# Attention weights and products in PSUM banks of their own, the product with v one turn later, and the reciprocal moved to the middle of the step

## Chip, cores and metric

The kernel runs on one core of a Trainium2 chip. The metric is the device time of one execution in microseconds (us). Before the change it was 1007.72 us (median of three runs, 1006.71 to 1010.24).

## What is computed

The reference chains two blocks. The first is attention over 8 batches x 8 heads, 576 positions, head width 64, that keeps only the 32 largest scores of each row:

```
scores = scale * (q @ k.T)
kth    = the 32nd largest score of each row
attn   = exp(where(scores >= kth, scores, -1e9) - max);  attn /= attn.sum() + 1e-9
out    = attn @ v
```

Its output, read as 4608 tokens of width 512, goes into a mixture of eight experts: each token takes the expert with the largest gate logit, each expert keeps the 80 tokens with the largest gate weight, applies `relu(x @ w1) @ w2`, and multiplies by the gate weight. All other rows of the output are zero. The change touches the attention block only.

## The kernel before

**Units and tiles.** Attention works on 32 head pairs, one after the other. A head pair has five tiles of query rows: tiles 0 to 3 of 128 rows, for both heads, and tile 4 of the last 64 rows, in which both heads share the 128 partitions. A unit is one head of one tile, so a head pair has nine units: two for each of the tiles 0 to 3, one for tile 4.

**The loop.** `run` (L454) lays out the program by hand (`manual_schedule`): each engine executes its instructions in the order in which they are written, and waits when an operand or a buffer isn't ready. `step(i)` (L473) is called once for each unit i and writes:

1. The loads of later q, k and v (L476 to 479, on SP's queue).
2. A string of letters (L488), one string for odd and one for even i, that interleaves VectorE work on several units: `G` a maximum over a sixth of a row (L250); `a` to `e` the rounds of the search for the 24th largest candidate (L261, L269), the last of which, `e`, also issues ScalarE's sign of the row against that candidate (L266); `y` GpSimd's product of the row with the sign (L272); `g` VectorE's maximum over that (L274); `h`/`H` the pick of the threshold (L277); `m`/`M` the mask of values below the threshold (L288), which for odd units is a ScalarE instruction (L293) and for even units a GpSimd one (L295). `h H m M` stand only in the string of even steps. `z`/`Z` is the reciprocal of the row sums (`over`, L360) and `x`/`X` the division of the product by the sums (`divide`, L370): two ScalarE copies with a scale (L385), except for tile 3, where VectorE does it (L377).
3. `turn_w` (L314) of a whole tile: TensorE transposes its scores into PSUM (L333) and adds the masks times a huge negative number (L339); ScalarE takes the exponential, first of the tail (the 65th to 128th key of the last chunk, L342), then of the rest (L343), into `wT`. Called *the turn* and *the exponentials* below.
4. `front` (L224): q times k of a later tile on TensorE (L234), and ScalarE's copy of the scores to SBUF (L242).
5. `back` (L346): the product of `wT` with v on TensorE (L356; 20 matmuls for a tile of two heads, 10 for tile 4), where v has a column of ones, so that the sums come with it. Called *the product*.
6. In some steps one more TensorE job that needs the PSUM tile of `front`: the transposes of q and k of the next head pair (`turn`, L211, ScalarE copy at L222), or, for the gate, the transposes of a finished head pair (L400, ScalarE copy L402). The gate logits (L407, copied at L414) are written inside `turn_w`, between its transposes and its masks (`gate`, L518).

With s = i mod 9, the tiles of these jobs are, before the change:

| s | turn | front | product | reciprocal, division | other |
|---|---|---|---|---|---|
| 7 | 0 | 1 | | 4 (of the pair before) | |
| 8 | | | 0 | | |
| 0 | 1 | 2 | | 0 | |
| 1 | | | 1 | | q, k transposes |
| 2 | 2 | 3 | | 1 | |
| 3 | | | 2 | | gate transposes |
| 4 | 3, logits in it | 4 | | 2 | |
| 5 | 4 | 0 | 3, ahead of the turn | | |
| 6 | | | 4 | 3 | |

Within a step the letters come first, then turn, front, product. Since nine is odd, the parity of i at a given s changes from one head pair to the next: where step 7 is odd, so are 0, 2 and 4, and 8, 1, 3 and 5 are even (called an *odd pair* below); in the next head pair it is the other way round (an *even pair*).

**PSUM** has eight banks. `ps_s` (L203) holds one tile of four banks for `front`, the transposes of q and k, and the gate; each use waits until ScalarE has copied the one before. `ps_w` is one tile of two banks for the turned scores `ab`. `ps_c` has two tiles `cc` of one bank; one `cc` holds the turned tail in its first 128 columns and behind them the products and sums of the same tile (L323, L351), and so lives from the turn until the division.

Of the kernel before, what the change touches and what calls it, by code (L numbers as in the profile page):

```python
# [9 lines left out]
F32 = mybir.dt.float32  # L10
# [4 lines left out]
Act = mybir.ActivationFunctionType  # L15
# [8 lines left out]
TINY = 2.0 ** -48  # L24
# [3 lines left out]
def kernel(  # L28
# [120 lines left out]
    class Attention:  # L149


        def __init__(self, stack, lean):
            self.lean = lean
            pool = lambda name, bufs, **kw: stack.enter_context(tc.tile_pool(name=name, bufs=bufs, **kw))
            self.nat, self.qkp, self.rows = pool("nat", 1), pool("qkp", 2), pool("rows", 2)
            self.small, vpool = pool("small", 7), pool("vpool", 1)
            self.ps_s, self.ps_w, self.ps_c = (pool(n, k, space=PSUM) for n, k in (("ps_s", 1), ("ps_w", 1), ("ps_c", 2)))
            self.qk, self.turned, self.lg = {}, {}, {}
            self.s, self.top, self.cnt, self.y, self.mask, self.w, self.xn = ({} for _ in range(7))
            self.both_s = {}  # L160
            self.thr, self.z = thr_all, z_all
            self.odd = set()


            self.vb = []
            for j in range(1 if lean else 3):
                t = vpool.tile([P, 3 * NF + 4, D + 1], F32, name=f"vb{j}")
                nc.gpsimd.memset(t[:, :, D : D + 1], 1.0)
                nc.gpsimd.memset(t[TL:, 3 * NF, :], 0.0)
                nc.gpsimd.memset(t[:TL, 3 * NF + 1 :, :], 0.0)  # L170
                self.vb.append(t)

            self.xT = vpool.tile([P, NK * P], F32, name="xT")
            nc.gpsimd.memset(self.xT[:, S:], 0.0)
# [139 lines left out]
        def turn_w(self, n, t, between=None):  # L314

            i = n * UPP + 2 * t
            g = 2 if t < NF else 1
            if i == NU - 1 and not self.lean:

                ab = self.four().rearrange("p h (c r) -> p h c r", r=P)  # L320
            else:
                ab = self.ps_w.tile([P, 2, NF, P], F32, name="ab", tag="ab")
            cc = self.ps_c.tile([P, 512], F32, name="cc", tag="cc")  # L323


            keys = [slice(c * P, c * P + P) for c in range(2 * NF + 1)] if t < NF else [slice(c * P, c * P + P) for c in range(NF)] + [slice(S - P, S)]
            dst = [ab[:, 0, c, :] for c in range(NF)] + [cc[:, :P]] + ([ab[:, 1, c, :] for c in range(NF)] if t < NF else [])
            sc, mk = self.both_s.pop((n, t)), self.mask.pop((n, t))
            for h in range(g):
                self.s.pop(i + h)  # L330

            for c, o in enumerate(dst):
                nc.tensor.matmul(o, lhsT=sc[:, keys[c]], rhs=ident, start=c in (0, NF, NF + 1), stop=False, is_transpose=True,  # L333
                                 skip_group_check=True)
            if between:
                between()

            for c in sorted(range(len(dst)), key=lambda c: c != NF):
                nc.tensor.matmul(dst[c], lhsT=mk[:, keys[c]], rhs=minus if self.lean else huge, start=False, stop=True,  # L339
                                 skip_group_check=True)  # L340
            wT = self.rows.tile([P, 2 * NF + 1, P], F32, name="wT", tag="wT")
            nc.scalar.activation(wT[:, 2 * NF, :], cc[:, :P], Act.Exp, scale=scale / TINY)  # L342
            nc.scalar.activation(wT[:, : g * NF, :], ab.rearrange("p h c r -> p (h c) r")[:, : g * NF, :], Act.Exp, scale=scale / TINY)  # L343
            self.w[n, t] = wT, cc

        def back(self, n, t):  # L346

            wT, cc = self.w.pop((n, t))
            vb = self.vb[n % len(self.vb)]
            for h in range(2 if t < NF else 1):  # L350
                o = slice(P + h * (D + 1), P + (h + 1) * (D + 1))  # L351
                for c in range(NK):
                    for r in range(0, P, TL):
                        j = h if t < NF else 2 * r // TL
                        k = j * NF + c if c < NF else 3 * NF + (h if t < NF else 2 + r // TL)
                        nc.tensor.matmul(cc[r : r + TL, o], lhsT=wT[:, h * NF + c if c < NF else 2 * NF, r : r + TL],  # L356
                                         rhs=vb[:, k, :], start=(c == 0), stop=(c == NF))
            self.w[n, t] = cc

        def over(self, n, t):  # L360


            g = 2 if t < NF else 1
            sums = self.w[n, t][:, P : P + 2 * (D + 1)].rearrange("p (h d) -> p h d", h=2)[:, :g, D]
            z = self.z[:, n % NP, t, :g]
            if self.lean:
                nc.vector.tensor_scalar(z, sums, EPS, None, op0=Alu.add)
            nc.vector.reciprocal(z, z if self.lean else sums)  # L368

        def divide(self, n, t):  # L370
            if t == 0:
                self.xn[n] = self.rows.tile([P, NK, 2, D], F32, name="xn", tag="xn")
            cc = self.w.pop((n, t))
            if t == NF - 1:

                sums = cc[:, P : P + 2 * (D + 1)].rearrange("p (h d) -> p h d", h=2)[:, :, :D]
                nc.vector.tensor_tensor(out=self.xn[n][:, t, :, :], in0=sums, op=Alu.mult,  # L377
                                        in1=self.z[:, n % NP, t, :].unsqueeze(2).to_broadcast([P, 2, D]))
                return
            for h in range(2):  # L380
                if t < NF:
                    p, o, j, m = slice(0, P), P + h * (D + 1), h, P
                else:
                    p, o, j, m = slice(TL * h, TL * h + TL), P, 0, TL
                nc.scalar.activation(self.xn[n][:m, t, h, :], cc[p, o : o + D], Act.Copy, scale=self.z[p, n % NP, t, j : j + 1])  # L385

        def norm(self, n, b, hp, bi, nb, cs=range(NK)):
# [66 lines left out]
        def run(self, slow):  # L454
# [8 lines left out]
            first, second = {}, {}  # L463
            later = []
            due = []
            drawn = []
            ready = {}

            def whole(i):

                return 0 <= i < NU and units[i][2] > 0

            def step(i, last):  # L473
                if 0 <= i < NU:
                    n, t, h = units[i]
                    if t == 2 and h == 1 and n + 2 < NP:  # L476
                        self.load(n + 2, *divmod(n + 2, HP))
                    if t == 3 and h == 1 and n + 2 < NP:
                        self.load_v(n + 2, *divmod(n + 2, HP))
                    if t in (1, 3) and h == 0 and slow and n:  # L480
                        slow.pop(0)()
                    if t == 0 and h == 0 and n + 1 < NP:
                        due.append(n + 1)
                    first[i] = self.parts(i)


                lag = dict(a=0, b=1, c=1, d=1, e=1, y=3, g=4, h=5, m=5, H=4, M=4)
                for c in "GybGcZGdXGeGGzaxg" if i % 2 else "GGbghHmMyGcZGdXGeGzax":  # L488
                    if c == "G":
                        if 0 <= i < NU:  # L490
                            next(first[i])
                    elif c == "a":
                        if 0 <= i < NU:
                            next(first[i], None)
                            second[i] = self.search(i)
                            next(second[i])
                    elif c in "zZxX":
                        for n, t in drawn:
                            if (t == NF - 1) == (c in "ZX"):
                                (self.over if c in "zZ" else self.divide)(n, t)  # L500
                    elif c in "mM":
                        if 0 <= i - lag[c] < NU:
                            self.below(i - lag[c])
                    elif i - lag[c] in second:
                        next(second[i - lag[c]])
                done = list(drawn)
                drawn.clear()

                def back():
                    if whole(i - LT - 1):  # L510
                        self.back(*units[i - LT - 1][:2])
                        drawn.append(units[i - LT - 1][:2])


                rest = whole(i - LT) and units[i - LT][2] == 2
                if rest:
                    back()
                def gate():  # L518
                    for g in later:
                        if ready[g] == 2:  # L520
# [2 lines left out]
                if whole(i - LT):  # L523
                    self.turn_w(*units[i - LT][:2], gate)

                ends = [(n, range(NK) if n < NP - 1 else range(NF) if t < NF else range(NF, NK))
                        for n, t in done if t == NF or (n == NP - 1 and t == NF - 1)]

# [1 line left out]
                busy = 0 <= f < NU and units[f][2] != 1  # L530
                if busy:
                    self.front(*units[f][:2])
                if not rest:
                    back()
                if due and not busy and i > 0:
                    self.turn(due.pop())
                    busy = True
# [413 lines left out]
```

## Time and profile before

| | |
|---|---|
| median of three runs | 1007.72 us |
| profiled execution | 1008.7 us, of which the span from first to last instruction is 1007.0 us |
| TensorE matmul busy | 857.1 us |
| VectorE busy | 811.3 us |
| ScalarE busy | 774.0 us |
| GpSimd busy | 625.8 us |
| granted TensorE clock | 0.98 on average |

The attention loop fills the span from about 30 to 876 us; the rest is routing and the experts. In the stretch from 500 to 600 us VectorE is busy for 91.32 us, ScalarE for 90.18 and TensorE for 87.23. Three engines are thus nearly full, and what counts is which waits for which. Three views tell it: the list of waits (who sat idle until whom, in total us, times and longest), the timeline of one engine in a window (start, length, line, and in brackets the idle time just before it with its releaser), and the groups by line. The release of a wait by an engine that is itself late tells where to look next.

### The profile page before, as it was taken

Reading aid. Unit: us, or ns where it says so; the run is one execution under the profiler, and the core shown is the slowest. Engines: PE = TensorE matmul, PEld = TensorE weight load, DVE = VectorE, ACT = ScalarE, POOL = GpSimd, SP = SyncE. Lnnn points to the kernel's source line nnn. Section 1 sums busy time; section 2 is a strip of 40 time slices with the busy share of each in tenths; the row PEclk is TensorE's granted clock in tenths of the full one; section 3 lists DMA queues with packets and bytes.
Section 4 is the critical chain, followed back from the end, with each engine's and each line's share of the span. In section 5 each row is a group of like instructions: output and inputs, shape, how many; then the busy total and the mean of one; then the engine's idle time right before and its main releaser. Section 6 shows DMA issues by size and latency. Waiting matters only on the chain.

```text
span 1007.0 us, 35335 instructions
## 1 busy us (share of the span) xinstructions
PE 857.1 (85%) x13112; PEld 690.6 (69%) x13112; DVE 811.3 (81%) x4960; ACT 774.0 (77%) x1588; POOL 625.8 (62%) x477
## 2 busy tenths in 40 slices
PE   5888898898888898888888888887888887689997
PEld 3666677676766677667666667666676676578886
DVE  5898999999898989898999999998999899361110
ACT  3889888898889898989898888898898989500110
POOL 3677677767677677677677776776767767301111
PEclk9999999999999999999999999999999999878999
DMA  3554443333323333333222221222221200183921
GB/s 86 129 140 125 131 131 91 89 97 97 98 76 85 96 93 86 98 97 77 55 56 55 56 54 45 51 50 56 56 55 44 58 22 14 33 316 127 388 73 31
DMA packets 189813, 91.00 MB, mean 90 GB/s; under 512 B 139712, under 2 KB 176576, under 8 KB 189632
## 3 DMA queue, kind: packets, MB, share of 16 engines
q1 hardware_dynamic: 188608, 86.03, 30.8%
q0 software_dynamic: 1024, 2.62, 0.8%
q8 instruction: 105, 1.72, 0.7%
q14 instruction: 76, 0.62, 0.2%
HBM read 68.44 MB, written 20.19 MB: 88 GB/s over the span
## 4 chain that ended last, share of the span: by engine, by line
PE 38%; ACT 25%; DVE 23%; issue 8%; POOL 3%; DMA 2%; POOLq 0%; ACTq 0%; DVEq 0%; SPq 0%
PE cc L356 12%; ACT sign L266 9%; DVE cand L250 7%; PE sp L234 6%; ACT wT L343 6%; DVE w L274 5%; PE sp L209 5%; ACT mask L293 4%; PE yp L835 4%; DVE cand L269 3%; ACT xn L385 3%; PE ab L333 3%; POOL y L272 3%; DVE top L261 2%; ACT wT L342 1%
## 5 line engine op out<-in xcount | busy, mean ns | idle before, releaser
L250 DVE MAX8 cand<-s 128x8 f32<-128x96 f32 x1728 | 400.2, 246 | 8.7 <-ACT s L242 8.7
L295 POOL TENSOR_SCALAR mask<-s,thr_all 128x576 bf16<-128x576 f32 x144 | 247.9, 1721 | 243.5 <-DVE pick L277 148.0
L272 POOL TENSOR_TENSOR y<-s,sign 128x576 f32<-128x576 f32 x288 | 363.1, 1281 | 12.7 <-ACT sign L266 12.7
L356 PEld LDWEIGHTS cc<-vb,wT 128*64 128x64 f32 x5760 | 184.1, 139 | 180.0 <-ACT wT L343 168.9
L356 PE MATMUL cc<-vb,wT 128*64 128x65 f32 x5760 | 206.5, 226 | 110.7 <-ACT wT L343 110.7
L274 DVE MAX8 w<-y 128x8 f32<-128x576 f32 x288 | 217.1, 754 | 14.6 <-POOL y L272 7.5
L266 ACT ACTIVATE sign<-s,w 128x576 bf16<-128x576 f32 x288 | 223.1, 775 | 6.6 <-DVE w L261 6.1
L234 PE MATMUL sp<-both 64*128 64x288 f32 (+1 forms) x1280 | 203.3, 437 | 9.8 <-ACT s L242 4.5
L242 ACT ACTIVATE s<-sp 128x1152 f32<-128x1152 f32 (+1 forms) x161 | 166.9, 1037 | 34.0 <-PE sp L234 32.6
L333 PE MATMUL ab<-ident,s 128*128 128x128 f32 x1148 | 178.7, 285 | 0.0
L343 ACT ACTIVATE wT<-ab 128x1024 f32<-128x1024 f32 (+1 forms) x159 | 149.9, 942 | 3.4 <-PE ab L339 3.2
L234 PEld LDWEIGHTS sp<-both 64*128 64x128 f32 (+1 forms) x1280 | 106.3, 180 | 51.0 <-ACT s L242 7.9
L333 PEld LDWEIGHTS ab<-ident,s 128*128 128x128 f32 x1148 | 130.1, 144 | 11.7 <-issue 0.8
L261 DVE MAX8 top<-cand 128x8 f32<-128x48 f32 x576 | 115.2, 200 | 5.6
L293 ACT ACTIVATE mask<-s,thr_all 128x576 bf16<-128x576 f32 x144 | 111.7, 776 | 8.3 <-DVE pick L277 7.9
L269 DVE MATCH_REPLACE8 cand<-top,cand 128x48 f32<-128x48 f32 x576 | 110.9, 192 | 0.0
L339 PE MATMUL ab<-huge,mask 128*128 128x128 bf16 x1148 | 91.2, 221 | 0.0
L339 PEld LDWEIGHTS <-mask 128*128 128x128 bf16 x1312 | 84.2, 99 | 7.2 <-issue 5.2
L368 DVE RECIPROCAL z_all<-cc 128x2 f32<-128x2 f32 (+1 forms) x160 | 25.8, 162 | 59.9 <-PE cc L356 59.9
L385 ACT ACTIVATE xn<-cc,z_all 128x64 f32<-128x64 f32 (+1 forms) x256 | 68.0, 306 | 1.6 <-DVE z_all L368 1.2
L222 ACT COPY both<-sp 128x1152 f32<-128x1152 f32 x31 | 34.8, 1123 | 30.0 <-PE sp L209 30.0
L342 ACT ACTIVATE wT<-cc 128x128 f32<-128x128 f32 x160 | 44.4, 278 | 17.0 <-PE cc L339 14.1
(187 smaller groups left out, 853.2 us busy)
## 6 DMA issues: line engine op xcount, KB each, us to landing
w<-in_moe_w_dram SPq DMA_DIRECT2D x10, 2048.0 KB, 12.3
vb<-in_v_dram SPq DMA_DIRECT2D x96, 128.0 KB, 2.7
w<-in_moe_w_dram SPq DMA_DIRECT2D x24, 512.0 KB, 3.8
out_dram<-zero SPq DMA_DIRECT2D x9, 1024.0 KB, 5.8
qn<-in_q_dram SPq DMA_DIRECT2D x64, 128.0 KB, 2.5
kn<-in_k_dram SPq DMA_DIRECT2D x64, 128.0 KB, 2.5
xd<-xn SPq DMA_DIRECT2D x32, 256.0 KB, 2.6
qn<-in_q_dram SPq DMA_DIRECT2D x32, 32.0 KB, 2.3
```

The costliest lines, as they stand in the source:

```text
L234: nc.tensor.matmul(o, lhsT=qT[d, t * P : t * P + m], rhs=kT[d, j * HS : (j + 1) * HS], start=True, stop=True)
L242: nc.scalar.activation(s[:, j * HS : (j + w) * HS].rearrange("p (j c) -> p j c", c=HS), ps[:, j : j + w, :HS], Act.Copy, scale=TINY)
L250: nc.vector.max(out=cand[:, j, :], in_=s[:, j * S // NG : (j + 1) * S // NG])
L266: nc.scalar.activation(sign, s, Act.Sign, bias=w9[:, 7:8], scale=-1.0, accum_out=cnt)
L272: nc.gpsimd.tensor_tensor(out=y, in0=s, in1=sign, op=Alu.mult)
L274: nc.vector.max(out=w9[:, 8:], in_=y)
L293: nc.scalar.activation(mask, self.s[i], Act.Relu, bias=self.thr[:, i : i + 1], scale=-1.0)
L295: nc.gpsimd.tensor_scalar(mask, self.s[i], self.thr[:, i : i + 1], None, op0=Alu.is_lt)
L333: nc.tensor.matmul(o, lhsT=sc[:, keys[c]], rhs=ident, start=c in (0, NF, NF + 1), stop=False, is_transpose=True, skip_group_check=True)
L339: nc.tensor.matmul(dst[c], lhsT=mk[:, keys[c]], rhs=minus if self.lean else huge, start=False, stop=True, skip_group_check=True)
L343: nc.scalar.activation(wT[:, : g * NF, :], ab.rearrange("p h c r -> p (h c) r")[:, : g * NF, :], Act.Exp, scale=scale / TINY)
L356: nc.tensor.matmul(cc[r : r + TL, o], lhsT=wT[:, h * NF + c if c < NF else 2 * NF, r : r + TL], rhs=vb[:, k, :], start=(c == 0), stop=(c = ...
```

## The change

- PSUM: the tail of the turn gets a pool and a bank of its own (`ps_t`, tile `tt`). `cc` now holds products and sums only, is allocated in `back`, and has one bank instead of two.
- `back` of a tile is written behind the next tile's `turn_w` and ahead of the step's `front`, by way of the list `turned`. The special case that put `back` ahead of the turn in step 5 is gone.
- The letters: `Z` and `X` are gone. For all tiles, `z` stands after the fourth `G` and `x` after the next one in even steps, and after the third and fourth `G` in odd steps. `e` moves behind the last `G`.
- The v of a later head pair is loaded one step later.

With these the table reads:

| s | turn | product | front | reciprocal, division | other |
|---|---|---|---|---|---|
| 7 | 0 | 4 (of the pair before) | 1 | | |
| 8 | | | | 4 (of the pair before) | |
| 0 | 1 | 0 | 2 | | |
| 1 | | | | 0 | q, k transposes |
| 2 | 2 | 1 | 3 | | |
| 3 | | | | 1 | gate transposes |
| 4 | 3, logits in it | 2 | 4 | | |
| 5 | 4 | 3 | 0 | 2 | |
| 6 | | | | 3 | |

Within a step the letters still come first, then turn, product, front. The numbers of instructions on each engine stay as they were.

```diff
-            self.ps_s, self.ps_w, self.ps_c = (pool(n, k, space=PSUM) for n, k in (("ps_s", 1), ("ps_w", 1), ("ps_c", 2)))
+            self.ps_s, self.ps_w, self.ps_t, self.ps_c = (pool(n, 1, space=PSUM) for n in ("ps_s", "ps_w", "ps_t", "ps_c"))
...
-            cc = self.ps_c.tile([P, 512], F32, name="cc", tag="cc")
+            tt = self.ps_t.tile([P, P], F32, name="tt", tag="tt")
...
-            dst = [ab[:, 0, c, :] for c in range(NF)] + [cc[:, :P]] + ([ab[:, 1, c, :] for c in range(NF)] if t < NF else [])
+            dst = [ab[:, 0, c, :] for c in range(NF)] + [tt] + ([ab[:, 1, c, :] for c in range(NF)] if t < NF else [])
...
-            nc.scalar.activation(wT[:, 2 * NF, :], cc[:, :P], Act.Exp, scale=scale / TINY)
+            nc.scalar.activation(wT[:, 2 * NF, :], tt, Act.Exp, scale=scale / TINY)
...
         def back(self, n, t):
-            wT, cc = self.w.pop((n, t))
+            wT = self.w.pop((n, t))
+            cc = self.ps_c.tile([P, 2 * (D + 1)], F32, name="cc", tag="cc")
...
-                    if t == 3 and h == 1 and n + 2 < NP:
+                    if t == NF and n + 2 < NP:
                         self.load_v(n + 2, *divmod(n + 2, HP))
...
-                for c in "GybGcZGdXGeGGzaxg" if i % 2 else "GGbghHmMyGcZGdXGeGzax":
+                for c in "GybGcGzdGxGGeag" if i % 2 else "GGbghHmMyGcGzdGxGea":
...
-                rest = whole(i - LT) and units[i - LT][2] == 2
-                if rest:
-                    back()
...
                 if whole(i - LT):
                     self.turn_w(*units[i - LT][:2], gate)
 
+                if turned and (whole(i - LT) or i >= NU + LT):
+                    self.back(*turned[0])
+                    drawn.append(turned.pop())
+                if whole(i - LT):
+                    turned.append(units[i - LT][:2])
...
                 if busy:
                     self.front(*units[f][:2])
-                if not rest:
-                    back()
```

## The prediction

> **What bounds the kernel now.** I read the list of waits first, then one stretch of the attention loop as timelines, engine by engine. The waits that touch the change:
>
> ```profile
> PEld cc L356 <- ACT wT L343: 168.9, 131, 3.5
> PE cc L356 <- ACT wT L343: 110.7, 98, 3.3
> DVE z_all L368 <- PE cc L356: 59.9, 67, 4.0
> ACT s L242 <- PE sp L234: 32.6, 54, 2.4
> ```
>
> TensorE's only large wait is that of the product for the exponentials (110.7 us), VectorE's only large one that of the reciprocal for the product (59.9 us). Both are what the change attacks. ScalarE waits little for the scores of `front` (32.6 us). A turn and a half on TensorE, from its timeline in an odd pair:
>
> ```profile
> 518.97 1.39 PE L356 MATMUL cc<-vb,wT 128*64 128x65 f32 x40 [0.63 <-ACT wT L343]
> 520.28 0.86 PE L209 MATMUL sp<-ident,qn 128*128 128x128 f32 x5
> 521.07 0.86 PE L209 MATMUL sp<-ident,kn 128*128 128x128 f32 x5
> 521.86 0.66 PE L333 MATMUL ab<-ident,s 128*128 128x128 f32 x4
> ...
> 522.96 0.61 PE L339 MATMUL ab<-huge,mask 128*128 128x128 bf16 x8
> 523.50 1.24 PE L234 MATMUL sp<-both 64*128 64x288 f32 x8
> 525.39 1.39 PE L356 MATMUL cc<-vb,wT 128*64 128x65 f32 x40 [0.66 <-ACT wT L343]
> ```
>
> Start to start, the product takes 1.31, the q, k transposes 1.58, the turn 1.64 (its masks some 0.6 of that), `front` 1.17 where the next job follows at once. ScalarE over the same stretch:
>
> ```profile
> 522.99 0.77 ACT L266 ACTIVATE sign<-s,w 128x576 bf16<-128x576 f32 x1
> ...
> 523.76 0.50 ACT L385 ACTIVATE xn<-cc,z_all 128x64 f32<-128x64 f32 x2
> 524.15 0.28 ACT L342 ACTIVATE wT<-cc 128x128 f32<-128x128 f32 x1
> 524.30 1.03 ACT L343 ACTIVATE wT<-ab 128x1024 f32<-128x1024 f32 x1
> 525.21 1.15 ACT L242 ACTIVATE s<-sp 128x1152 f32<-128x1152 f32 x1
> 526.22 0.81 ACT L293 ACTIVATE mask<-s,thr_all 128x576 bf16<-128x576 f32 x1
> ```
>
> Sign 0.76 with its read, division 0.39, exponentials 1.06, score copy 1.01, mask 0.67. The reader is to see the fit: `front` (1.17) runs beside the exponentials (1.06), so the score copy never waits here and frees the scores' PSUM tile during the product. The third bound is a loop between VectorE and GpSimd, seen on GpSimd in an even pair:
>
> ```profile
> 541.93 1.72 POOL L295 TENSOR_SCALAR mask<-s,thr_all 128x576 bf16<-128x576 f32 x1 [1.31 <-DVE pick L277]
> 543.62 2.52 POOL L272 TENSOR_TENSOR y<-s,sign 128x576 f32<-128x576 f32 x2
> 547.45 1.72 POOL L295 TENSOR_SCALAR mask<-s,thr_all 128x576 bf16<-128x576 f32 x1 [1.31 <-PE sp L209]
> ```
>
> Mask to mask is 5.52 us for two steps: mask, two products, VectorE's maximum and picks, next mask. No change to TensorE's order can go below it.
>
> **Baseline.** VectorE's division of tile 3 (L377) starts at 507.39, 533.03 and 560.10, so an odd and an even pair together take 52.71 us, 26.36 each. The sum below is made in these double pairs; the loop has 32 head pairs, so I count 15.5 double pairs. It is set against the profiled execution, 1008.7 us (span 1007.0); the median of the runs is 0.1% below it.
>
> **Part by part.** (1) Banks of their own: no instruction more or less. The tail shared its bank only with the product that waits for its exponential anyway; I take 0 us. But `cc` goes from two tiles to one: each product now waits for the division before it, a ScalarE instruction for four of five tiles. (2) The product behind the next turn: its 110.7 us of waiting go, since its exponentials are a turn old. What is late next is `front`: it now ends 1.31 + 1.17 after the turn while the exponentials end 1.06 after it, so the score copy waits up to 1.4 us in each turn, with all of ScalarE's queue behind it (mask, division, sign), unless TensorE is ahead by that much. And where a job for the scores' PSUM tile follows (q, k transposes in step 1, gate transposes in step 3), nothing stands on TensorE between `front` and it: it waits for the whole score copy, 1.01 plus 0.15, which the product used to cover. (3) Reciprocal and division in mid-step: 160 and 256 instructions as before. Reciprocals of tiles 0, 1 and 2 come half a step later than before, those of tile 3 a little later or earlier, but their products come a whole turn later. (4) `e` two `G` later: 2 x 0.165 us, in a queue where the sign's user is a step away: 0. (5) v one step later: its six DMAs land in 2.7 us and the first use is over nine steps (25 us) away: 0; were that cover gone, the first product of each head pair would wait.
>
> **The loop that closes.** I follow what each job waits for, with these durations, 0.10 from TensorE to ScalarE and 0.15 back (a score copy began at 509.05 where `front` had let the next job start at 508.93; a product began at 514.15 where the exponentials had at 513.98). From the end of tile 0's score copy (step 5) to the same a head pair later:
>
> Odd pair. Mask 0.67, hand-over 0.15, mask matmuls of turn 0 0.62, product 4 0.74, front 1.17 + 0.10, score copy 1.02: 4.47. Mask 0.67 + 0.15 (behind that copy in ScalarE's queue, needed by turn 1), mask matmuls 0.62, product 0 1.32, front 1.17 + 0.10, copy 1.02: 5.05. Hand-over 0.15, q, k transposes 1.58, turn 2 1.64, product 1 1.32, front 1.17 + 0.10, copy 1.02: 6.98. Then ScalarE's mask 0.67, division 0.40, sign 0.75, gate copy 0.53, hand-over 0.15, logits 0.69, mask matmuls of turn 3 0.62, product 2 1.32, front 1.17 + 0.10, copy of tile 4 0.56: 6.96. Mask 0.67, division of tile 2 0.40, which frees `cc`, 0.15, product 3 1.32, front 1.17 + 0.10, copy 1.02: 4.83. Sum **28.29 us**.
>
> Even pair, where the masks come a step earlier and don't bind: sign 0.75, mask 0.67, sign 0.75, exponentials 1.08, 0.15, turn 1 1.64, product 1.32, front 1.17 + 0.10, copy 1.02: 8.65. The q, k part, 6.98. Then 0.15, gate transposes 0.79, turn's transposes 1.03, logits 0.69, masks 0.62, product 1.32, front 1.17 + 0.10: 5.87. Copy of tile 4 0.56, division 0.40, 0.15, product 1.32, front 1.17 + 0.10, copy 1.02: 4.72. Sum **26.22 us**.
>
> Together 54.51, against 52.71 now: the two engines alone, waiting for nobody else, are 1.80 us slower per double pair. VectorE adds to it. In an odd pair, product 3 ends so late that the reciprocal of tile 3, now early in step 6, waits for it. From there: reciprocal 0.27, rest of step 6 1.75 (five short maxima and replaces, the division 0.19, the long maximum 0.66), two steps at the GpSimd loop's 5.52, 2.66 to the `w` that the sign of step 0 needs (516.51 to 518.84 in the timeline, and two `G` more), 0.10, sign 0.75, exponentials 1.08, score copy 1.02: 13.15. TensorE and ScalarE alone need 2.29 + 8.65 = 10.94 for it. So 2.2 us more, 56.7 in all: 4.0 us per double pair, x 15.5 = 62, and 1008.7 + 62 = **1071 us**.
>
> The Trainium skill, "Perfetto Trace Analysis", section "Matmuls" under "Optimizing Tensor Performance", says that independent matmul groups should rotate through different PSUM banks so that the evacuation of one overlaps the next; that speaks against the single `cc`. By that rule alone the loss would be the wait of product 3 for the division: 1.88 from front to product instead of the 0.97 of turn 4 in odd pairs and 1.21 instead of 0.97 in even ones, an estimate of 18 us; the trace before has no wait on `cc` to compare.
>
> **Rivals.** (a) TensorE and ScalarE close the loop, but VectorE catches up in the even pair (its stretch there is slack, the reciprocals of tiles 1 and 2 not being on the loop): 1.80 x 15.5 = 28, 1037 us. For it: in the two pairs read, VectorE waits no more than 1.33 us at that reciprocal now. (b) On the other side: TensorE runs ahead. It loses 110.7 us of waits, and in even pairs it idles 1.06 to 1.72 before three of five products, as much as the product that is put ahead of `front`. If that lead survives step 1 and step 3, `front` is done when the exponentials are, the reciprocals' 59.9 us go too, and the GpSimd loop sets the pace: 4.5 x 5.52 = 24.8 per head pair, 1.5 x 31 = 47 us less, 962 us; half of it, 985. It decides from the point where TensorE is 1.4 us ahead of ScalarE at every turn; against it, two jobs per head pair wait for a score copy and take that lead away, and ScalarE is idle for only 9.8 us of the 100 from 500 to 600. (c) The change doesn't do what it says, because waits only trade places and both loops come out even: 54.51 would have to be 52.7, 3% in my hand-overs: 1000 to 1015 us.
>
> **Chances.** Loop with VectorE's detour 0.55 (1055 to 1095: the same detour in the odd pair too would be 2.2 x 15.5 = 34 more, 1105, of which I let in two thirds, since there the masks already hold TensorE back); (a) 0.27 (1020 to 1055); (b) 0.11; (c) 0.07. About 0.3%, 3 us, is what a measurement of this kernel can tell from no change. Slower 0.86, within 0.3% 0.03, faster 0.11. The range takes in the first two, with a little below the second: 1025 to 1095.
>
> **What would show it.** Right: the product's wait for the exponentials (110.7) nearly gone; ScalarE's wait at L242 for `front` up from 32.6 to over 100 us; TensorE waits of about 1 us before L209 on the score copy, and a wait of the product on the division; VectorE's wait at the reciprocal as large as before or larger, mostly in steps 5 and 6; double pairs of 55 to 57 us. Wrong: L242's wait stays near 30 us, or the reciprocals no longer wait: then (b). If the loop is right but the reciprocal of tile 3 doesn't hold the next head pair, double pairs are near 54.5: (a).

## The result, and the profile after

The changed kernel takes **1085.8 us** (median of four runs, 1082.46 to 1090.32) against 1007.3 beside it: 1.0776 times the time of before, interval 1.0731 to 1.0821. Its profiled execution took 1082.46 us with a span of 1080.7. The forecast was 1071.

The list of waits of the changed kernel (engine, line, waited for: total us, times, longest), where L357 is the product (L356 before), L369 the reciprocal (L368) and L386 the division (L385):

```profile
DVE z_all L369 <- PE cc L357: 133.7, 71, 3.1
ACT s L242 <- PE sp L234: 129.9, 117, 2.4
...
PE sp L209 <- ACT s L242: 86.8, 61, 2.5
...
PE ab L333 <- ACT wT L343: 33.6, 17, 4.1
PE tt L339 <- ACT mask L293: 27.8, 33, 0.9
...
PE cc L357 <- ACT xn L386: 17.0, 32, 0.8
```

The product no longer waits for exponentials (110.7 us before). The larger waits that took its place on the three engines are in this list: VectorE's for the product has doubled (59.9), ScalarE's for `front` quadrupled (32.6), and TensorE now waits for the score copy ahead of the q, k and gate transposes (L209), for the exponentials of the turn before ahead of the next turn (L333), for ScalarE's mask ahead of the mask matmuls (L339), and for the division ahead of a product. An odd pair on TensorE (idle time and releaser in brackets):

```profile
505.33 0.86 PE L209 MATMUL sp<-ident,qn 128*128 128x128 f32 x5 [1.23 <-ACT s L242]
...
508.55 1.39 PE L357 MATMUL cc<-vb,wT 128*64 128x65 f32 x40
509.86 1.24 PE L234 MATMUL sp<-both 64*128 64x288 f32 x8
512.34 0.86 PE L209 MATMUL sp<-ident,xn 128*128 128x128 f32 x5 [1.23 <-ACT s L242]
...
520.31 1.39 PE L357 MATMUL cc<-vb,wT 128*64 128x65 f32 x40 [0.85 <-ACT xn L386]
```

and the other two engines at the same time, ScalarE:

```profile
511.15 1.13 ACT L242 ACTIVATE s<-sp 128x1152 f32<-128x1152 f32 x1 [1.16 <-PE sp L234]
...
518.54 0.65 ACT L242 ACTIVATE s<-sp 128x576 f32<-128x576 f32 x1 [1.42 <-PE sp L234]
```

VectorE:

```profile
517.42 0.17 DVE L369 RECIPROCAL z_all<-cc 128x2 f32<-128x2 f32 x1 [1.99 <-PE cc L357]
521.74 0.17 DVE L369 RECIPROCAL z_all<-cc 128x2 f32<-128x2 f32 x1 [1.55 <-PE cc L357]
```

Read them as a loop. The product at 508.55 stands ahead of `front`, so the score copy starts at 511.15 after 1.16 us of nothing on ScalarE; the gate transposes wait 1.23 us for that copy; everything behind them, product 2 included, is late, and VectorE stands at its reciprocal for 1.99 us. From the start of one score copy of tile 0 to the next, all odd head pairs but the first take 28.51 us. Even pairs take 28.76 to 30.08, and none of them is undisturbed: each of the 15 full ones holds 3.4 us in which the granted TensorE clock is 0.5. An even pair put together from parts of two pairs that no such stretch touches takes 28.44 us (an estimate; the parts are shown below). A double pair at full clock thus takes about 56.95 us; before, by the divisions of tile 3, it was 52.71.

### The profile page after: what moved, and what is told of

The parts are those of the page before. It is cut to its first block, busy times and chain, and to the rows that moved or that the text cites. A ratio compares the mean times of both kernels' runs of the same rounds, so it can differ in the third digit from the quotient of the medians.

```text
span 1080.7 us, 35404 instructions
## 1 busy us (share of the span) xinstructions
PE 878.5 (81%) x13112; PEld 705.0 (65%) x13112; DVE 816.8 (76%) x4960; ACT 778.5 (72%) x1588; POOL 625.7 (58%) x477
## 5 line engine op out<-in xcount | busy, mean ns | idle before, releaser
L250 DVE MAX8 cand<-s 128x8 f32<-128x96 f32 x1728 | 379.4, 246 | 8.9 <-ACT s L242 8.8
L272 POOL TENSOR_TENSOR y<-s,sign 128x576 f32<-128x576 f32 x288 | 363.0, 1282 | 12.7 <-ACT sign L266 12.7
L242 ACT ACTIVATE s<-sp 128x1152 f32<-128x1152 f32 (+1 forms) x161 | 166.0, 1031 | 129.9 <-PE sp L234 129.9
L357 PE MATMUL cc<-vb,wT 128*64 128x65 f32 x5760 | 207.5, 227 | 17.7 <-ACT xn L386 17.0
L333 PE MATMUL ab<-ident,s 128*128 128x128 f32 x1148 | 188.6, 295 | 33.6 <-ACT wT L343 33.6
L357 PEld LDWEIGHTS cc<-vb,wT 128*64 128x64 f32 x5760 | 185.3, 140 | 37.5 <-ACT xn L386 22.5
L333 PEld LDWEIGHTS ab<-ident,s 128*128 128x128 f32 x1148 | 136.6, 149 | 78.2 <-ACT wT L343 47.9
L369 DVE RECIPROCAL z_all<-cc 128x2 f32<-128x2 f32 (+1 forms) x160 | 26.1, 163 | 134.9 <-PE cc L357 133.7
L339 PEld LDWEIGHTS <-mask 128*128 128x128 bf16 x1312 | 88.4, 103 | 37.4 <-POOL y L272 18.0
L339 PE MATMUL ab<-huge,mask 128*128 128x128 bf16 x1148 | 95.9, 228 | 0.0
L209 PE MATMUL sp<-ident,qn 128*128 128x128 f32 (+1 forms) x160 | 28.6, 292 | 54.0 <-ACT s L242 49.9
L386 ACT ACTIVATE xn<-cc,z_all 128x64 f32<-128x64 f32 (+1 forms) x256 | 69.0, 311 | 4.0 <-DVE z_all L369 3.6
L209 PEld LDWEIGHTS sp<-ident,qn 128*128 128x128 f32 (+1 forms) x160 | 18.4, 144 | 74.1 <-ACT s L242 64.3
```

The lines of the kernel that those rows point to most:

```text
L242: nc.scalar.activation(s[:, j * HS : (j + w) * HS].rearrange("p (j c) -> p j c", c=HS), ps[:, j : j + w, :HS], Act.Copy, scale=TINY)
L250: nc.vector.max(out=cand[:, j, :], in_=s[:, j * S // NG : (j + 1) * S // NG])
L272: nc.gpsimd.tensor_tensor(out=y, in0=s, in1=sign, op=Alu.mult)
```

## Experiments

The first four runs take the change apart. **The banks alone** (the kernel before with `tt`, and `cc` of one tile allocated in `back`):

```diff
-            cc = self.ps_c.tile([P, 512], F32, name="cc", tag="cc")
+            tt = self.ps_t.tile([P, P], F32, name="tt", tag="tt")
...
-            wT, cc = self.w.pop((n, t))
+            wT = self.w.pop((n, t))
+            cc = self.ps_c.tile([P, 2 * (D + 1)], F32, name="cc", tag="cc")
```

> The kernel before with the banks of the change alone: tail in a bank of its own, one tile for products and sums, allocated in back; order and letters as before. Theory A: each product waits for its own exponentials anyway, which stand behind the division of the tile before in ScalarE's queue, so the single tile costs nothing: 1002 to 1013 us. Rival C: a product waits for a division and the time is above 1030 us.

Measured: 1008.17 us, ratio 0.9993 (0.9976 to 1.0009). With the old order the single `cc` costs nothing that can be measured.

**The letters alone** (the kernel before):

```diff
-                for c in "GybGcZGdXGeGGzaxg" if i % 2 else "GGbghHmMyGcZGdXGeGzax":
+                for c in "GybGcGzdGxGGeag" if i % 2 else "GGbghHmMyGcGzdGxGea":
```

> The kernel before with the letters of the change alone: reciprocal and division of all tiles in the middle of the step, e behind the last G; banks and product as before. Theory A: the reciprocal stands 0.6 to 0.8 us earlier behind the same product, VectorE waits longer there (59.9 us up to 80 to 150), but ScalarE and TensorE set the pace; 1005 to 1035 us. Rival B: the letters make most of the loss, 1050 us or more.

Measured: 1002.63 us, ratio 0.9944 (0.992 to 0.9969): faster, which neither theory had. The reciprocal waits a little longer (68.4 us). But VectorE is busy for 798.6 us instead of 811.3 with the same instructions. The gain sits in the even pairs: without a half-clock stretch they take 26.55 us instead of 27.01, odd ones 25.69 as against 25.70. VectorE's group of short maxima (busy us, mean ns of one) has to be read with care:

```profile
L250 DVE MAX8 cand<-s 128x8 f32<-128x96 f32 x1728 | 379.8, 246 | 8.7 <-ACT s L242 8.6
```

The mean is the 246 ns of before and the busy time is 20 us less than the 400.2 of before. That isn't 20 us less work. Where two instructions of a group overlap, its busy time counts the overlap once, and a short maximum overlaps with an instruction of another group just as well. Two places in VectorE's timeline of before:

```profile
501.28 0.24 DVE L250 MAX8 cand<-s 128x8 f32<-128x96 f32 x1
501.44 0.07 DVE L269 MATCH_VALUE_LOAD cand<-top,cand 128x8 f32 x1
...
502.49 0.41 DVE L250 MAX8 cand<-s 128x8 f32<-128x96 f32 x2
```

In both, the instruction behind a maximum starts 0.16 to 0.17 us after it. Which neighbours make the 12.7 us of all VectorE work isn't shown.

**The order alone** (the kernel before, its banks and letters):

```diff
+                if turned and (whole(i - LT) or i >= NU + LT):
+                    self.back(*turned[0])
+                    drawn.append(turned.pop())
+                if whole(i - LT):
+                    turned.append(units[i - LT][:2])
...
-                if not rest:
-                    back()
```

> The kernel before with the order of the change alone: product a turn late, behind the next turn and ahead of front, v one step later; two tiles cc and the letters as before. Theory A: this carries most of the loss, 1050 to 1095 us, with ScalarE's wait for front near 130 us. Rivals B and C: 1000 to 1030 us.

Measured: 1206.18 us, ratio 1.1937 (1.1904 to 1.1969), far above what any of the theories expected. The late product carries the loss, and more than all of it. ScalarE waits 218.6 us for `front`, VectorE 244.2 for products, and TensorE 123.3 us at L333 for divisions: `cc` of before is held from the turn to the division, which is now three steps later, and the tail of the turn after next wants the same tile. So the banks and letters must win back what the order loses. **Undoing the banks in the changed kernel** asks for their share (the diff of the banks, backwards):

> The changed kernel with the banks of before: two tiles cc of one bank that hold tail and products together. Each cc then lives from the turn to the division three steps later, and the tail of the turn after next waits for that division (123.3 us at L333 in the run with the order alone). If the banks are what carries the late product: 1120 to 1200 us. If the letters are what made the difference between the order alone (1206 us) and the whole change (1086 us): 1080 to 1100 us.

Measured: 1156.73 us, ratio 1.1447 (1.1419 to 1.1476): the banks carry 71 us, and the wait at L333 for divisions is back (71.8 us). Part of the 71 us comes with a lower clock, 0.93 instead of 0.96. **Undoing the letters** (changed order and banks, old strings):

> The changed kernel with the letters alone undone: late product in the new banks, reciprocal and division at the end of the step for all tiles but tile 3. Theory A2: the single cc must be free for the next product, and a division at the end of the step comes to ScalarE behind its sign; the product waits for it: 1080 to 1130 us. If the early reciprocals of tiles 0, 1, 2 and 4 are what costs: under 1065 us.

Measured: 1116.15 us, ratio 1.1044 (1.1024 to 1.1065), with 56.6 us of product waiting for division instead of 17.0. **Undoing the order** (banks and letters, product and loads as before):

> The changed kernel with the order alone undone: banks and letters as changed, product of a tile behind its own exponentials as before (and v loaded as before). If the late product carries the whole loss: as the letters alone, 998 to 1008 us, faster than the kernel before by about 0.6%. If banks and letters cost something together: above 1015 us.

Measured: 1006.62 us, ratio 0.9974 (0.9964 to 0.9984). The eight combinations, as ratios to the kernel before timed beside each: none 1; banks 0.9993; letters 0.9944; banks and letters 0.9974; order 1.1937; order and letters 1.1447; order and banks 1.1044; all 1.0776. Nothing that has the late product comes near 1, and nothing without it is slower than 1.

The other runs ask why. **Front ahead of the late product**:

```diff
-                if turned and (whole(i - LT) or i >= NU + LT):
-                    self.back(*turned[0])
-                    drawn.append(turned.pop())
-                if whole(i - LT):
-                    turned.append(units[i - LT][:2])
...
                 if busy:
                     self.front(*units[f][:2])
+                if turned and (whole(i - LT) or i >= NU + LT):
+                    self.back(*turned[0])
+                    drawn.append(turned.pop())
+                if whole(i - LT):
+                    turned.append(units[i - LT][:2])
```

> The changed kernel with one thing turned round: in each step front is written ahead of the product (turn, front, product), the product still a turn late, banks and letters as changed. Theory A (the loss is that the product stands ahead of front, so that the score copy comes late and with it all of ScalarE's queue, and that nothing covers the score copy ahead of the q, k and gate transposes): front runs beside the exponentials again and the product covers the score copy; ScalarE's wait for front falls from 129.9 us to under 50, TensorE's waits for the score copy ahead of L209 (86.8) to under 20, and the time falls to 970 to 1010 us. Rival B (the early reciprocals are the loss): they stay early, so 1050 us or more, with VectorE's wait at the reciprocal still over 100 us. Rival C (the single bank for products is the loss): 1050 us or more, with the product waiting for the division.

Measured: 1114.84 us, ratio 1.1043 (1.1016 to 1.1071). Theory A fell in this form. The wait it was about did go, ScalarE's for `front` from 129.9 to 30.4 us, but TensorE's ahead of L209 fell only to 58.6, and the time rose. The time and VectorE's wait for products, 172.5 us, are what rival B had expected; against the early reciprocals as the whole loss stands the run above with the letters undone, which is slower than the change. Rival C's sign is missing: the product waits 1.3 us for divisions. Where VectorE waits, TensorE of this run shows, and then VectorE:

```profile
503.56 2.18 PE L234 MATMUL sp<-both 64*64 64x288 f32 x8 [1.53 <-ACT part L415]
505.68 2.43 PE L357 MATMUL cc<-vb,wT 128*64 128x65 f32 x40
```

```profile
508.16 0.17 DVE L369 RECIPROCAL z_all<-cc 128x2 f32<-128x2 f32 x1 [4.78 <-PE cc L357]
```

In step 4, `front` needs the PSUM tile that ScalarE frees with the copy of the gate logits, and that copy stands behind a sign that waits for VectorE. The product, now behind `front`, waits with it, and VectorE waits for the product: the loop closes over VectorE. The clock was halved in this stretch as well: `front` and product are 2.18 and 2.43 us long instead of 1.19 and 1.39, which is 2.0 of the 4.78 us. In odd pairs at full clock front first is a gain, 26.8 to 26.9 us instead of 28.51. The loss sits in the even pairs, 30.2 to 34.7 us, each with 3.4 to 10.2 us at half clock. **Front first in all steps but step 4** takes this one place away:

```diff
+                gated = whole(i - LT) and units[i - LT][1] == NF - 1
+                if turned and gated:
+                    self.back(*turned[0])
+                    drawn.append(turned.pop())
...
                 if busy:
                     self.front(*units[f][:2])
+                if turned and (whole(i - LT) or i >= NU + LT) and not gated:
+                    self.back(*turned[0])
+                    drawn.append(turned.pop())
```

> The changed kernel with front ahead of the late product in all steps but step 4, where product 2 stays ahead. In the run with front first everywhere, front of tile 4 waited 1.5 us for ScalarE's copy of the gate logits, which stands behind a sign that waits for VectorE, and product 2 behind it was waited for by VectorE for up to 4.8 us. Theory: that loop is why front first lost; without it 1020 to 1075 us, less than the change. If front first loses anyway, because every product then comes 1.17 us later to its reciprocal: 1090 us or more.

Measured: 1073.19 us, ratio 1.0609 (1.0572 to 1.0647): 42 us from one place in nine steps, and less than the change. How much of the 42 us is that wait and how much the clock (0.93 in the one run, 0.94 to 0.96 in the other) is not separated. Pairs at full clock take 27.37 us (odd) and 28.41 (even), 55.78 together, 1.2 less than in the changed kernel. With the **reciprocal and division at the end of the step** on top (strings `GybGcGdGGGezaxg` and `GGbghHmMyGcGdGGezax`):

> The same with reciprocal and division of all tiles at the end of the step after their product, still ahead of the next product. Theory A2: with the reciprocal 0.6 to 0.9 us later its waits shrink, and cc is free in time: 990 to 1045 us and less than the run before it. If the division behind the sign holds up the next product: above the run before it.

Measured: 1050.84 us, ratio 1.0393 (1.0371 to 1.0415): less again, though 6 us above the range. VectorE's wait for products falls from 146.4 to 108.8 us, and the double pair at full clock from 55.78 to 54.58 (26.71 and 27.87).

**The reciprocal of tile 3 alone at the end of step 6**, all else as changed (`Z`, `X` for tile 3):

```diff
-                for c in "GybGcGzdGxGGeag" if i % 2 else "GGbghHmMyGcGzdGxGea":
+                for c in "GybGcGzdGxGGeagZX" if i % 2 else "GGbghHmMyGcGzdGxGeaZX":
```

> The changed kernel with reciprocal and division of tile 3 alone moved to the end of step 6. If that reciprocal is the joint at which the late product 3 holds VectorE up, as the prediction has it (2.2 us in a double head pair): 1045 to 1065 us. If the wait of tile 2's reciprocal one step earlier takes its place: 1075 to 1090 us.

Measured: 1065.19 us, ratio 1.0546 (1.053 to 1.0561), at the upper end of the first range. The five even pairs at full clock take 27.01 us instead of the 28.44 estimated for the changed kernel, odd pairs 28.50, as there. That is the detour of the prediction, taken away by itself: it was to be 2.2 us, in the even pair alone, and is about 1.4, there alone.

**Holding the reciprocal back to the next step with a turn**, behind the sign (`e`) of that step, once with the changed order, once with front first:

```diff
+                turns = whole(i - LT) or i >= NU + LT
...
-                for c in "GybGcGzdGxGGeag" if i % 2 else "GGbghHmMyGcGzdGxGea":
+                for c in "GybGcGdGGGezaxg" if i % 2 else "GGbghHmMyGcGdGGezax":
...
-                        for u in drawn:
+                        for u in drawn if turns else ():
...
-                done = list(drawn)
-                drawn.clear()
+                done = list(drawn) if turns else []
+                if turns:
+                    drawn.clear()
```

> The changed kernel (product a turn late, ahead of front; new banks) with reciprocal and division held back to the end of the next step that has a turn, behind e, so that they stand one to two steps behind their product. Theory A2 (a loop of TensorE and ScalarE, plus a detour over VectorE: a product that comes late in one step is asked for by the reciprocal in the middle of the next, VectorE stops there, the sign and with it the exponentials come late, and so the next product): VectorE's wait at the reciprocal falls from 133.7 us to under 40, what is left is the loop of TensorE and ScalarE, 1035 to 1060 us. Theory F (front behind the product is all): 1075 to 1095 us, no better than the change. If the reciprocal was all of it: under 1010 us.

> Both at once: front ahead of the late product, and reciprocal and division held back to the end of the next step with a turn. Theory A2: the score copy runs under the product, the reciprocal finds its product done; TensorE no longer waits for the exponentials (110.7 us before) and VectorE hardly for products: 970 to 1005 us, faster than the kernel before. Theory that front first does harm by itself, as its 1114.84 us with early reciprocals could be read: 1060 us or more.

Measured: 1171.27 us, ratio 1.1581 (1.156 to 1.1602), and 1063.08 us, ratio 1.0532 (1.0497 to 1.0568). Theory A2 fell in both, and so did theory F in the first. The second time lies where the rival theory, that front first does harm by itself, had put it. The waits of the first of the two runs show what happened:

```profile
ACT s L242 <- PE sp L234: 227.0, 144, 3.5
DVE z_all L369 <- PE cc L357: 200.8, 65, 5.4
...
PE cc L357 <- ACT xn L386: 122.8, 88, 4.1
```

With one `cc`, the next product can't start before the division, and the division now stands behind the sign of the same step. The product waits 122.8 us, and in the first run `front` behind it; in the second the product waits 64.8 us. Front first by itself does no harm here: between the two runs it gains 108 us. Between product and division the late product leaves only a narrow place: too early, and VectorE waits; too late, and the next product does.

## Why the prediction was right, point by point

- **What bounds.** Right. The two waits that the change attacks behaved as said, one gone, the other doubled.
- **The loop.** The sums were 28.29 us for the odd pair and 26.22 + 2.2 = 28.4 for the even one; odd pairs took 28.51. For the even pair at full clock, ScalarE's score copies of two pairs give the parts, first of a pair ahead of its half-clock stretch, then of another behind its own:

```profile
464.50 1.13 ACT L242 ACTIVATE s<-sp 128x1152 f32<-128x1152 f32 x1 [1.31 <-PE sp L234]
...
469.62 1.13 ACT L242 ACTIVATE s<-sp 128x1152 f32<-128x1152 f32 x1
...
475.27 1.14 ACT L242 ACTIVATE s<-sp 128x1152 f32<-128x1152 f32 x1
```

```profile
418.32 1.13 ACT L242 ACTIVATE s<-sp 128x1152 f32<-128x1152 f32 x1 [0.22 <-PE sp L234]
...
425.32 1.13 ACT L242 ACTIVATE s<-sp 128x1152 f32<-128x1152 f32 x1 [0.50 <-PE sp L234]
...
432.27 0.65 ACT L242 ACTIVATE s<-sp 128x576 f32<-128x576 f32 x1 [1.42 <-PE sp L234]
...
435.99 1.14 ACT L242 ACTIVATE s<-sp 128x1152 f32<-128x1152 f32 x1 [1.25 <-PE sp L234]
```

Start to start that is 5.12 and 5.65, then 7.00, 6.95 and 3.72: 28.44 us. The single waits came at the places named: TensorE 1.23 us ahead of the q, k and of the gate transposes, ScalarE up to 1.4 us ahead of its score copy, product 3 0.85 us for the division in odd pairs and 0.18 in even ones (0.91 and 0.24 in the prediction's estimate). VectorE's detour was summed to 13.15 us from the reciprocal of tile 3 to the end of the score copy in step 0; in the pair above it takes 13.01, from the reciprocal

```profile
463.27 0.17 DVE L369 RECIPROCAL z_all<-cc 128x2 f32<-128x2 f32 x1 [1.59 <-PE cc L357]
```

to 476.28, where ScalarE's next instruction starts behind the copy of 475.27. That the detour is part of the loop is shown by the run with tile 3's reciprocal late. Without it the even pair takes 27.01, where the sum for TensorE and ScalarE alone was 26.22; what fills these 0.8 us isn't shown, and rival (a) didn't come.
- **Rivals (b) and (c).** TensorE didn't run ahead (b): ScalarE waits 129.9 us for `front`, and TensorE 86.8 us for the score copy ahead of L209, which the prediction had named as what would take the lead away. That waits only trade places (c) didn't come either.
- **What the runs corrected.** The prediction's words made `front` behind the product the core. Turning the two round alone made the time longer. The loss is that of the whole loop, in which each job's lateness reaches the next product by one of three ways (score copy, division, reciprocal); closing one way shifts the load to another. Shown is that the late product is needed for the loss and that each of the three ways carries part of it; that they are all there is isn't shown, since the clock changes with the order. Which order of jobs would let a late product pay is left open. 1050.84 us was the best found, and its double pair at full clock (54.58) is still 1.9 us longer than before.
- **Banks and letters.** Item (1) put the banks of their own at 0. With the old order that holds (1008.17 us); with the late product they save 71 us. Items (3) and (4) gave the letters no price. Alone they gain 6 us, with the late product 30. The forecast is a sum for the whole change and didn't need these terms.
- **Clock: not in the sum.** The spans differ by 73.7 us (1080.7 and 1007.0), the sum had 62. Fifteen double pairs at 56.95 instead of 52.71 us make 63.6. The rest is the clock: over 28.44 us the 15 even pairs lose 17.7 us together, and in the trace before five even pairs lose 6.7 over their 27.01, so 11 us more; the first odd pair, shorter in both, takes 0.8 off. The profiled execution is the fastest of the four, and the median lies 3.3 us above it. Two even pairs of the changed kernel in three stretches each (start:end and length, us; busy time and instructions of PE, PEld, DVE, ACT, POOL; then the granted clock, the DMA share and GB/s):

```profile
407.23:417.23 10.00, 8.16 (x106) 7.09 (x107) 9.42 (x60) 8.84 (x18) 6.39 (x5) 0.83 0.44 123
417.23:427.23 10.00, 7.54 (x89) 5.60 (x87) 8.19 (x50) 8.71 (x16) 6.24 (x5) 1.00 0.44 106
427.23:435.99 8.76, 8.57 (x146) 6.77 (x146) 6.93 (x47) 6.10 (x17) 5.64 (x4) 1.00 0.05 17
```

```profile
464.50:474.50 10.00, 7.63 (x112) 6.15 (x111) 9.74 (x64) 8.83 (x18) 6.38 (x5) 1.00 0.46 118
474.50:484.50 10.00, 7.30 (x76) 5.89 (x76) 6.73 (x41) 7.50 (x13) 6.23 (x5) 0.83 0.44 125
484.50:494.47 9.97, 9.30 (x150) 7.33 (x151) 8.14 (x55) 7.30 (x20) 5.60 (x4) 1.00 0.01 3
```

Both meet one stretch at half clock of 3.4 us. In the first pair it starts at 412.94 and falls on turn 1, while ScalarE's sign waits for VectorE anyway; the pair takes 28.76 us, 0.3 more than at full clock. In the second it starts at 477.79 and falls on turn 2, on the loop, and the pair takes 29.97, 1.5 more. The reader finds it on TensorE as the q, k transposes after their wait and a turn that takes 3.07 us (478.12 to the product at 481.19) instead of 1.64:

```profile
476.46 0.86 PE L209 MATMUL sp<-ident,qn 128*128 128x128 f32 x5 [2.49 <-ACT s L242]
...
478.12 1.11 PE L333 MATMUL ab<-ident,s 128*128 128x128 f32 x4
...
481.19 1.39 PE L357 MATMUL cc<-vb,wT 128*64 128x65 f32 x40
```

So the clock makes nearly all of the difference between the sum and the span. That the pairs differ only in this, and the 28.44 us with it, is read from pairs of one trace, not from a run that keeps the clock up, which wasn't made.

## What to carry to other kernels

To move a consumer one turn later removes its wait, but on engines that execute in written order it moves every wait behind it: write down what stands behind it in each queue, which buffer lives longer for it, and who asks for its result next, and add up the loop from a buffer's release to the same release one period later. Here that sum, made with start-to-start times of the trace before, came within 1% of the period after at full clock (56.7 against 56.95 us); it had no term for a clock that answers to the new waits. Of the whole change only the letters are worth keeping: the kernel before with the letters alone takes 1002.63 us and beats both.

## What the runs showed of the hardware

TensorE's clock answers to a new pattern of waits even where TensorE is busy for about 80% of the time (85% of the span before, 81% in the changed kernel, 77% with the order alone). The trace before has five stretches of 3.4 us at half clock up to the end of attention, and so have those of the banks alone, the letters alone and both. The changed kernel has 16 (one of them 6.8 us long), the order alone 36 (11 of them 6.8 us long), and the mean granted clock goes from 0.98 to 0.963 and 0.924. Some follow waits of only 2.27 us (at 528.67) and 2.49 us (at 476.46). The stretches start on a raster: those at 412.94, 477.79 and 528.99 us lie 19 and 15 times 3.413 us apart. The Trainium skill, "TensorE: Matmul & The Clock Gate", section "Part 1: The HAM clock gate", has the clock halve after at least one idle window of about 3.4 us; the length of the stretches agrees with that window, the waits ahead of them are shorter than it. TensorE alone in the 3.41 us ahead of these three stretches, and in one more (start:end and length, busy time and matmuls, granted clock, DMA share and GB/s):

```profile
409.53:412.94 3.41, 1.57 (x12) 1.00 0.55 125
474.37:477.79 3.42, 1.33 (x9) 1.00 0.15 56
525.57:528.99 3.42, 1.15 (x11) 1.00 0.54 120
467.55:470.96 3.41, 1.57 (x16) 1.00 0.58 128
```

It was busy for a third to nearly half of each. The last was followed by no half-clock stretch, though as busy as the first, so the busy time alone doesn't tell which one is.

And short VectorE instructions overlap with what stands behind them: a maximum of 0.24 us at 501.28 has the next instruction start at 501.44. So the busy time of a group (1728 maxima of 246 ns each: 400.2 us in one interleaving, 379.8 in the other) doesn't tell what an interleaving saves.
